# Transposing q and k of every stage on TensorE, with three prepared and two transposed buffers

## The chip, the cores and the metric

The kernel runs on one core of one Trainium2 chip. The metric is the device time of one execution in microseconds (us); the time given for a kernel is the median of several executions. A profiled execution has a time of its own, and inside it a span, from its first to its last recorded instruction.

## The reference

Two computations follow each other. The first is a linear attention with a decaying state, for 4 batches and 8 heads, 768 time steps, head dimension 48:

```python
for t in range(S):
    kt, vt, rt = k[:, :, t], v[:, :, t], r[:, :, t]
    cur = einsum('bhd,bhe->bhde', u[None] * kt, vt)
    y[:, :, t] = einsum('bhd,bhde->bhe', rt, state + cur)
    state = w[None, :, :, None] * state + einsum('bhd,bhe->bhde', kt, vt)
```

Its result, laid out as 3072 tokens of 384 numbers, goes through two dense layers with a leaky ReLU between them:

```python
h = x @ w_in                    # 3072 x 384 by 384 x 2048
g = maximum(0.01 * h, h)
out = g @ w_out                 # 2048 x 384
```

Inputs and output are float32; the kernel multiplies in bfloat16.

## The kernel before, in words

**Stages.** The time steps are cut into chunks of 128, six for each batch, so 24 stages `n` in all. A stage is one `front(n)` and one `back(n)`, and its loads are made by `load(n)`.

- `load(n)` (L409 to L416) issues three loads of 128 x 384 float32, for r, k and v, into one of `NRAW` = 4 raw buffers each. All are issued from SyncE (SP). A load waits until the stage that used the raw buffer four stages earlier has read it. From stage `NXQ` on it has one wait more (L415, `after=`): for the k product of stage n - `GATE`, two stages earlier.
- `front(n)` multiplies r and k by decay tables on VectorE into `qk_h` (q at L424, k at L426), and casts v to bfloat16 on ScalarE (L428). `qk_h` and `v_sb` have `NPREP` buffers. VectorE then makes the bonus term of u: two products and a sum (L430, L432, L434), from which GpSimd makes `vs` (L436).
- q and k are then transposed into `qkT`, which has `NT` buffers. There are two ways, and `n < NXQ` (L448) chooses. The first is eight 128 x 128 TensorE transposes into the PSUM bank `p_t` (L445), then one ScalarE copy of 128 x 1024 to `qkT` (L450). There is one `p_t` bank. The second is one transposing DMA from SBUF to SBUF, issued from SP (L453).
- From `qkT` come eight matmuls of the chunk's own attention (L460), masked on VectorE in two instructions (L465). k and v give the chunk's state update (L473 on TensorE, L481, L484 and L486 on VectorE).
- `back(n)` multiplies q by the state (L495) and the masked attention by v (L501), both on TensorE. VectorE adds `vs` (L507), TensorE transposes the result (L511), and ScalarE writes it to `xT` (L516).

**The dense layers.** `g1` (L572, evicted with the leaky ReLU by ScalarE at L577) and `g2` (L592, evicted by ScalarE at L596, stored from SP at L598) work on token tiles: eight of 128 tokens, then four of 512. They take turns in `NMOE` = 3 PSUM banks, which the small transpose of L511 shares. Twelve ScalarE casts (L533) bring `w_in` to bfloat16 in the first stages; `w_out` is loaded with a cast from GpSimd (L538).

**Order of the work.** The program isn't run in the order of its text. Every operation has a duration that the author wrote down and a priority; `Prog.schedule` (L116) plays the program through with these and writes down one fixed order for each engine. Stage work has a priority of about 100 n, dense work of over 100000, so that TensorE takes dense work when no stage work is ready. On the chip each engine then keeps its order, and waits on semaphores. A change of one buffer count or of one route therefore gives all engines a new order.

Of the kernel before, what the change touches and what calls it, by code (L numbers as in the profile page):

```python
# [26 lines left out]
TILES = [(L * i, L) for i in range(NSMALL)] + [(512 * i, 512) for i in range(NSMALL // 4, 6)]  # L27
NRAW = 4
FILL = (0.0, 0.0, 215.0)
NT = 3  # L30
GATE = 2
NXQ = 8
NXY = 24
WIN_AT = [0, 1, 2, 3]
WOUT_AT = [3, 4, 5, 6]
CAST = [20, 118, 160, 218]
RANK = {"q": 2, "k": 3, "v": 4, "bonus": 5, "vs": 7, "T": 8, "Tev": 9, "A": 10, "mask": 11, "kv": 10, "Z": 12, "S": 12,
        "qs": 14, "av": 14, "y": 15, "xt": 16, "xev": 17}
NPREP = 4
NGT = 3  # L40
NOUT = 3
NMOE = 3
# [21 lines left out]
class Prog:  # L64
# [10 lines left out]
    def op(self, eng, fn, dur, prio, w=(), r=(), banks=(), dma=None, svc=0, lock=False, grp=None, after=()):  # L75
        o = Op()
        o.eng, o.fn, o.dur, o.prio, o.dma, o.svc, o.lock, o.grp = eng, fn, dur, prio, dma, svc, lock, grp
        if grp is not None:
            if eng == "PE" and grp.first is None:
                grp.first = o  # L80
            grp.last = o
        o.idx = len(self.ops)
        o.name = str(list(w)[:1])
        o.deps = set()
        o.raw = set()
        for k in after:
            o.deps.add(self.writer[k])
        for k in r:
            if k in self.writer:
                o.deps.add(self.writer[k])  # L90
                o.raw.add(self.writer[k])
        for k in w:
            if k in self.writer:
                o.deps.add(self.writer[k])
                if self.writer[k].dma or eng != "PE":
                    o.raw.add(self.writer[k])
            for x in self.readers.get(k, ()):
                o.deps.add(x)
                if eng != "PE":
                    o.raw.add(x)  # L100
        for k in r:
            self.readers.setdefault(k, []).append(o)
        for k in w:
            self.writer[k] = o
            self.readers[k] = []
        for b in banks:
            last = self.bank.setdefault(b, {})
            for e, x in last.items():
                if e != eng:
                    o.deps.add(x)  # L110
            last[eng] = o
        o.deps.discard(o)
        self.ops.append(o)
        return o
# [179 lines left out]
def bass_rwkv5_eagle__then__act_leaky_relu_kernel(nc, r, k, v, w, u, moe_w_in, moe_w_out, out):  # L294
# [3 lines left out]
    def SB(name, shape, dt=BF16):  # L298
        return ctx.enter_context(nc.sbuf_tensor(name, shape, dt))
# [28 lines left out]
    raw_v = [SB(f"raw_v{i}", [128, H, D], FP32) for i in range(NRAW)]  # L328
    v_sb = [SB(f"v_sb{i}", [128, H, D]) for i in range(NPREP)]
    qk_h = [SB(f"qk_h{i}", [128, 2, H, E]) for i in range(NPREP)]  # L330
    q_h = [t[:, 0, :, :] for t in qk_h]
# [4 lines left out]
    vs = [SB(f"vs{i}", [128, H, D], FP32) for i in range(2)]  # L336
    qkT = [SB(f"qkT{i}", [128, 2, NP, L]) for i in range(NT)]
    ATm = [[SB(f"ATm{i}_{p}", [128, NP, L]) for p in range(2)] for i in range(2)]
# [58 lines left out]
    for p in range(2):  # L397
# [4 lines left out]
                                      w_tab[:, :, :], ALU.mult), 490, -80, w=["uw"], r=["w", gu], grp=gu)  # L402
    for i in range(NPREP):
        op("DVE", lambda i=i: V.memset(q_h[i][:, :, D:E], 0.0), 100, -60 + i, w=[f"qpad{i}"])
# [4 lines left out]
    def load(n):  # L409
        b, c = divmod(n, NC)  # L410
        ri = n % NRAW
        for j, (x, raw, nm) in enumerate(((r, raw_r, "rr"), (k, raw_k, "rk"), (v, raw_v, "rv"))):
            src = x[b].rearrange("h t d -> t h d")[c * L:c * L + L, :, :]
            op("SP", lambda src=src, raw=raw: [SP.dma_start(raw[ri][:, :, :], src)], 650, order[0],
               w=[f"{nm}{ri}"], after=[f"k{(n - GATE) % NPREP}"] if n >= NXQ else [], dma=(f"{nm}{ri}", 16), svc=1000)  # L415
            order[0] += 1  # L416

    def front(n):
        b, c = divmod(n, NC)
        ri, pi, di = n % NRAW, n % NPREP, n % 2  # L420
        base = n * 100
# [17 lines left out]

        T, ti = qkT[n % NT], n % NT  # L440
        gt = Group("t")
        def tr():
# [4 lines left out]
            return last  # L447
        if n < NXQ:  # L448
            op("PE", tr, 450, base + RANK["T"], w=[gt], r=[f"q{pi}", f"k{pi}", f"qpad{pi}", f"kpad{pi}", "ident"], grp=gt)
# [39 lines left out]
    def back(n):  # L489
        b, c = divmod(n, NC)  # L490
        pi, di, sc, base = n % NPREP, n % 2, n % 3, n * 100
        T, ti, vv = qkT[n % NT], n % NT, v_sb[pi]
        def qs():
            for i in range(NP):
                last = PE.matmul(p_y[:, 2 * D * i:2 * D * i + 2 * D], T[:, 0, i, :], s_bd[sc][:, i, :],  # L495
                                 start=(i == 0), stop=False, skip_group_check=True)
            return last
# [164 lines left out]
```

## Time and profile before

| | before |
|---|---|
| executions | 185.98, 187.28, 187.28 us |
| median | 187.28 us |
| profiled execution, its own time | 185.98 us |
| its span | 184.3 us |
| TensorE busy | 162.6 us (88%) |
| VectorE busy | 113.7 us (62%) |
| ScalarE busy | 111.7 us (61%) |
| GpSimd busy | 25.7 us (14%) |
| granted TensorE clock, mean | 0.991 |

In what follows PE is TensorE, PEld its weight loads, DVE VectorE, ACT ScalarE, POOL GpSimd. A group of instructions is given by line, engine, operation and tiles, followed by its count, its busy time in us and the mean of one in ns, then the idle time of the engine before it with what ended that. The busy time of a TensorE instruction holds its way through the array, so that instructions in a row overlap: what one costs in a row is read from the starts, or from the chain of waits, which counts nothing twice.

### The profile page before, as it was taken

The numbers are of one execution on the slowest core, as the hardware profiler recorded it, in microseconds if no ns is written. First come the engines' busy times: TensorE is split into PE (matmuls) and PEld (weight loads), VectorE is DVE, ScalarE is ACT, GpSimd is POOL, SyncE is SP. The second block draws the span as 40 slices with busy tenths as digits, with TensorE's granted clock in tenths as the row PEclk, the third lists the DMA queues.
The fourth block names the chain that finished last, engine by engine and source line by source line (L and its number), as shares of the span: only waits on it lengthen the run. The fifth ranks groups of instructions, "written<-read, shape, count | busy, mean of one in ns | idle before, by whom it ended". The sixth has DMA issues, their size and how long they took to land.

```text
span 184.3 us, 3981 instructions
## 1 busy us (share of the span) xinstructions
PE 162.6 (88%) x1632; PEld 105.7 (57%) x1642; DVE 113.7 (62%) x242; ACT 111.7 (61%) x196; POOL 25.7 (14%) x36
## 2 busy tenths in 40 slices
PE   0448488796999999999998999999999999999993
PEld 0227367686976668875554555665645654466561
DVE  2388758795999899999999999998600000000000
ACT  3877998995864147556677678632895149912221
POOL 2011111222112111111111211223000000000000
PEclk9999979999999999999999999999999999999999
DMA  3999999999659999999999989797000220012122
GB/s 84 252 218 233 263 276 180 205 201 218 129 108 229 207 230 222 203 189 231 231 176 223 220 163 227 143 161 184 7 0 0 85 78 13 0 43 85 52 80 85
DMA packets 97988, 28.25 MB, mean 153 GB/s; under 512 B 92721, under 2 KB 95922, under 8 KB 97970
## 3 DMA queue, kind: packets, MB, share of 16 engines
q1 hardware_dynamic: 96976, 26.42, 66.2%
q0 software_dynamic: 576, 1.57, 5.1%
q8 instruction: 13, 0.21, 0.5%
q10 hardware_dynamic: 418, 0.00, 0.1%
q14 instruction: 5, 0.04, 0.1%
HBM read 20.65 MB, written 4.72 MB: 138 GB/s over the span
## 4 chain that ended last, share of the span: by engine, by line
PE 76%; ACT 13%; DMA 6%; DVE 2%; issue 1%
PE p_moe L592 34%; PE p_moe L572 29%; DMA raw_v<-in_v_dram 4%; ACT w_in_sb L533 4%; PE p_a L460 3%; ACT gS L577 2%; PE p_y L501 2%; PE p_y L495 2%; ACT qkT L450 2%; DMA w_tab<-in_w_dram 2%; PE p_moe L511 2%; PE p_t L445 1%; PE p_z L473 1%; PE p_moe L383 1%; ACT xT L516 1%
## 5 line engine op out<-in xcount | busy, mean ns | idle before, releaser
L572 PE MATMUL p_moe<-xT,w_in_sb 128*128 128x128 bf16 (+1 forms) x566 | 74.5, 277 | 5.0 <-ACT w_in_sb L533 2.7
L572 PEld LDWEIGHTS p_moe<-xT,w_in_sb 128*128 128x128 bf16 x576 | 41.5, 101 | 23.9 <-ACT w_in_sb L533 4.2
L592 PE MATMUL p_moe<-w_out_sb,gT 128*128 128x384 bf16 x256 | 44.5, 326 | 0.5 <-ACT gT L577 0.5
L577 ACT ACTIVATE gT<-p_moe 128x512 bf16<-128x512 f32 x64 | 38.2, 597 | 10.6 <-PE p_moe L572 8.2
L596 ACT ACTIVATE o_sb<-p_moe 128x384 f32<-128x384 f32 x24 | 11.8, 491 | 41.2 <-PE p_moe L592 41.2
L436 POOL TENSOR_TENSOR vs<-v_sb,s_b 128x384 f32<-128x384 bf16 x24 | 22.0, 917 | 93.4 <-DVE s_b L434 54.8
L592 PEld LDWEIGHTS p_moe<-w_out_sb,gT 128*128 128x128 bf16 x256 | 24.6, 98 | 16.7 <-ACT gT L577 0.6
L592 PE MATMUL p_moe<-w_out_sb,gS 128*128 128x384 bf16 x128 | 24.2, 326 | 0.0
L577 ACT ACTIVATE gS<-p_moe 128x512 bf16<-128x512 f32 x32 | 18.4, 603 | 2.7 <-PE p_moe L572 2.5
L507 DVE TENSOR_TENSOR y_sb<-p_y,vs 128x384 bf16<-128x384 f32 x24 | 13.3, 553 | 8.2 <-PE p_y L501 8.1
L465 DVE TENSOR_TENSOR ATm_0<-p_a,mask_f 128x512 bf16<-128x512 f32 x24 | 16.4, 685 | 2.1 <-PE p_a L460 1.8
L424 DVE TENSOR_TENSOR qk_h<-raw_r,qdec 128x384 bf16<-128x384 f32 x24 | 14.5, 604 | 4.2 <-DMA raw_r<-in_r_dram 4.2
L465 DVE TENSOR_TENSOR ATm_1<-p_a,mask_f 128x512 bf16<-128x512 f32 x24 | 16.3, 679 | 0.0
L426 DVE TENSOR_TENSOR qk_h<-raw_k,kdec 128x384 bf16<-128x384 f32 x24 | 15.9, 661 | 0.3 <-ACT wlm L398 0.3
L428 ACT ACTIVATE v_sb<-raw_v 128x384 bf16<-128x384 f32 x24 | 12.5, 521 | 4.8 <-DMA raw_v<-in_v_dram 4.8
L592 PEld LDWEIGHTS p_moe<-w_out_sb,gS 128*128 128x128 bf16 x128 | 11.6, 98 | 6.3
L516 ACT ACTIVATE xT<-p_moe 128x384 bf16<-128x384 bf16 x24 | 11.8, 490 | 4.6 <-PE p_moe L511 4.4
L533 ACT ACTIVATE w_in_sb<-gT 128x512 bf16<-128x512 f32 x12 | 12.7, 1131 | 1.2 <-DMA gT<-in_moe_w_in_dram 1.2
L434 DVE TENSOR_REDUCE s_b<-qku 128x8 f32<-128x384 bf16 x24 | 13.1, 546 | 0.3
L445 PE MATMUL p_t<-ident,qk_h 128*128 128x128 bf16 x64 | 5.7, 242 | 7.9 <-DVE qk_h L426 7.9
L460 PE MATMUL p_a<-qkT 64*128 64x128 bf16 x192 | 10.0, 226 | 2.3 <-ACT qkT L450 2.2
L432 DVE TENSOR_TENSOR qku<-qk,uw 128x384 bf16<-128x384 bf16 x24 | 11.0, 458 | 0.4
(43 smaller groups left out, 125.3 us busy)
## 6 DMA issues: line engine op xcount, KB each, us to landing
raw_r<-in_r_dram SPq DMA_DIRECT2D x24, 192.0 KB, 3.5
raw_k<-in_k_dram SPq DMA_DIRECT2D x24, 192.0 KB, 4.0
raw_v<-in_v_dram SPq DMA_DIRECT2D x24, 192.0 KB, 4.1
out_dram<-o_sb SPq DMA_DIRECT2D x24, 192.0 KB, 2.0
gT<-in_moe_w_in_dram SPq DMA_DIRECT2D x4, 768.0 KB, 6.0
w_out_sb<-in_moe_w_out_dram POOLq DMA_DIRECT2D x4, 384.0 KB, 5.4
qkT<-qk_h SPq DMA_TRANSPOSE x16, 3.7
w_tab<-in_w_dram SPq DMA_DIRECT2D x1, 192.0 KB, 3.5
```

Source lines behind the costliest of these rows:

```text
L424: op("DVE", lambda: V.tensor_tensor(qh[:, :, 0:D], rr[:, :, :], qdec[:, :, :], ALU.mult), 490, base + RANK["q"], w=[f"q{pi}"], r=[f"rr{ri} ...
L426: op("DVE", lambda: V.tensor_tensor(kh[:, :, 0:D], rk_[:, :, :], kdec[:, :, :], ALU.mult), 490, base + RANK["k"], w=[f"k{pi}"], r=[f"rk{ri ...
L434: op("DVE", lambda: V.tensor_reduce(s_b[di][:, :], qku[di][:, :, :], AX.X, ALU.add), 470, base + RANK["bonus"], w=[f"s{di}"], r=[f"qku{di}"])
L436: op("POOL", lambda: G.tensor_tensor(vs[di][:, :, :], vv[:, :, :], s_b[di][:, :].unsqueeze(2).to_broadcast([128, H, D]), ALU.mult), 790, b ...
L460: last = PE.matmul(p_a[p][:, 128 * i:128 * i + 128], T[64 * p:64 * p + 64, 1, i, :], T[64 * p:64 * p + 64, 0, i, :], start=True, stop=True)
L465: op("DVE", lambda p=p: V.tensor_tensor(ATm[di][p][:, :, :], p_a[p][:, :].rearrange("p (i t) -> p i t", t=L), mask_f[:, :].unsqueeze(1).to ...
L507: op("DVE", lambda: V.tensor_tensor(y_sb[di][:, :], p_y[:, 0:DM], vs[di][:, :, :].rearrange("p h d -> p (h d)"), ALU.add), 490, base + RAN ...
L516: op("ACT", lambda: ACT.activation(xT[:, :, L * n:L * n + L], moe16(gx)[:, 0:DM].rearrange("p (m t) -> p m t", t=L), AF.Copy), 370, base + ...
L533: op("ACT", lambda m=m: ACT.activation(w_in_sb[:, m, CH * i:CH * i + CH].rearrange("p (j q) -> p j q", j=4), w_st[i][:, m, :].rearrange("p ...
L572: op("PE", lambda m=m, fb=fb, gr=gr: PE.matmul(p_moe[gr.bank][:, nt * (fb % per):nt * (fb % per) + nt], w_in_sb[:, m, 128 * fb:128 * fb + ...
L577: op("ACT", lambda f0=f0, gr=gr: ACT.activation(gb[:, f0:f0 + per, :], p_moe[gr.bank][:, :].rearrange("p (f t) -> p f t", t=nt), AF.Lrelu) ...
L592: op("PE", lambda q=q, fb=fb, gr=gr: PE.matmul(p_moe[gr.bank][:, 0:DM], gb[:, fb, 128 * q:128 * q + 128], w_out_sb[:, fb, :], start=(fb == ...
```

## The change

Three constants change:

```diff
-NT = 3
+NT = 2
 GATE = 2
-NXQ = 8
+NXQ = 24
 NXY = 24
...
-NPREP = 4
+NPREP = 3
```

`NXQ` = 24 is the number of stages. All stages now take the TensorE way of L445 and L450, where 16 took the transposing DMA of L453. The same constant switches the additional wait of the loads (L415): no stage has it any more, and a load waits for its raw buffer alone. `NT` = 2 leaves two buffers for the transposed q and k, and `NPREP` = 3 leaves three for the prepared q, k and v (the loop of padding memsets at L403 runs three times instead of four). What is computed does not change. Since the order of every engine is planned anew, dense and stage work are interleaved in another way from stage 7 on.

## The prediction

> **What bounds the kernel now.** I read the page first (busy shares), then busy time by stretch, then the waits, then the chain of waits.
>
> ```profile
> 0.00:46.00 46.00, 28.48 (x409) 23.36 (x409) 31.03 (x76) 36.38 (x54) 8.72 (x18) 0.96 0.98 213
> 46.00:52.00 6.00, 5.87 (x113) 5.49 (x113) 5.67 (x12) 5.53 (x11) 1.66 (x2) 1.00 0.62 124
> 52.00:130.40 78.40, 77.42 (x814) 48.91 (x823) 74.65 (x152) 45.47 (x90) 15.37 (x16) 1.00 0.99 195
> 130.40:184.30 53.90, 50.80 (x302) 27.96 (x304) 2.31 (x4) 24.28 (x44) 0.00 (x0) 1.00 0.12 45
> ```
>
> Columns: stretch, length, busy us (count) of PE, PEld, DVE, ACT, POOL, clock, DMA share, GB/s. Four regimes: a head in which PE idles; a short passage; stages 8 to 23, with PE (99%) and DVE (95%) both nearly full; and dense work alone, where PE has no gap. ACT is at 58% in the third.
>
> ```profile
> POOL vs L436 <- DVE s_b L434: 54.8, 13, 10.3
> ACT o_sb L596 <- PE p_moe L592: 41.2, 20, 2.9
> ...
> PE p_t L445 <- DVE qk_h L426: 7.9, 2, 7.2
> ACT v_sb L428 <- DMA raw_v<-in_v_dram: 4.8, 4, 2.1
> ...
> PE p_a L460 <- ACT qkT L450: 2.2, 4, 0.9
> ```
>
> These are waits: total us, times, longest. PE's own waits nearly all lie in the head; asked for 46 us onward, PE has only 0.5 and 0.2 us. No wait names the transposing DMA (L453): nobody stands visibly behind it.
>
> ```profile
> 49.00 0.20 PE p_y L501 x8
> 49.20 0.62 PE p_moe L572 x11
> 49.81 0.45 PE p_t L445 x8
> 50.26 0.17 PE p_z L473 x4
> ...
> 139.80 10.40 PE p_moe L592 x64
> 150.20 0.05 issue
> 150.25 10.31 PE p_moe L572 x47
> 160.56 20.82 PE p_moe L592 x128
> 181.37 0.02 issue
> 181.40 0.49 ACT o_sb L596
> ```
>
> From the chain of waits: from 46 us to the end it is PE in a row. One stage's eight transposes take 0.45 us there (56 ns each), and 64 dense matmuls of 384 columns take 10.40 us (163 ns). PE ends at 181.40; one eviction and one store follow, 2.9 us to the end of the span.
>
> **What the Trainium skill says.** "TensorE: Matmul & The Clock Gate", Part 4: PE-mode transpose, gives about 275 ns for a 128 x 128 transpose in a kernel. The trace's records (median 219 ns) are of that size, but they are latencies; in a row one costs 56 ns, which I use. "SBUF — State Buffer", Who interferes with whom, states that DMA never contends with a compute engine, so I expect no faster PE or DVE from fewer DMAs; the trace fits, with full-rate L592 matmuls at a DMA share of 1.0. The same section: a DVE instruction with two SBUF inputs contends with a GpSimd instruction that reads SBUF. The trace agrees: L432, 0.35 us alone, takes 0.87 us beside L436. "DMA: Bandwidth & Descriptors", Latency and other measured facts, gives 261 GB/s for transposing DMAs, an estimate of 1.0 us for the 262 kB of a stage; here it takes 3.7 us from issue to landing, so the measurement holds.
>
> **The change part by part.**
>
> *Transposes on PE.* 16 stages x 0.45 = 7.2 us more PE work. I listed both planned PE orders and priced each entry from the chain (L572 56 and 217 ns, L592 163, L501 25, L460 41, L495 and L473 43, transposes 55): 153.2 before, 160.2 us after, +7.0. There is no cover: PE has dense work waiting until the end.
>
> *Evictions on ACT.* 16 x 1.02 us (L450) = 16.4 us. ACT is busy 45.5 of 78.4 us in the third stretch; 61.9 of 78 (79%) fits. By the new order the tightest pair of stages (7 and 8) has about 4.4 us of ACT work between two transposed tiles, with DVE at about 4.3 to 5.7. Cost zero in the main case; if this cover fails, PE waits for L450, as in the head: 2.2 us in 4 of 8 stages, mean 0.28. Upper bound 16 x 0.28 = 4.4 us.
>
> *The DMA transposes leave.* 16 issues on SP, 1.3 to 3.8 us each, and 3.7 us of latency go. SP's loads and stores follow sooner. Nobody waited there, so the gain is nil in itself. What is late next: each stage now needs k product, transposes, L450, L460 in turn, about 0.45 + 1.02 + 0.4 us and handovers, near 2.1 us against 3.7.
>
> *The loads' second wait goes.* Stage 8's first load, issued at 41.25 us, could go at about 40.2, after stage 7's last. Behind loads that wait for reads of stage n - 4 stand stores on SP; three output buffers, with 2.6 us of PE work each, cover that. Gain between 0 and 2.1 us (the longest wait for `raw_v`, which belongs to stage 7, issued earlier): I take 0. The first transposing DMA comes at 56 us, so the head, where PE is idle, loses no work of any kind; up to stage 7's L460 (51.6 us) both PE orders are the same entry by entry.
>
> *Three and two buffers.* DVE can't work ahead as far. Before, it does so once: 11.3 us of PE work lie between the L460 of stages 7 and 8, with q and k of three stages done meanwhile. After, it is 3.5 us. So attention goes evenly, and DVE's pace counts in each stage. A full DVE stage takes 4.97 us in the trace (79.80 to 84.77, no gap). Pricing both DVE orders with the pieces of that stage (0.47 each for L424, L426, L484, L507; 0.6 for each L465; 0.46, 0.33, 0.28, 0.27 for L434, L430, L432, L486; 0.5 for the GpSimd block): from the masks of stage 7 to those of stage 23, 76.0 us before and 75.0 after. In the new order several L434 are followed by PSUM work that GpSimd doesn't block, so 73.3 is possible.
>
> *The sum.* In that same passage PE has 76.6 us of work before and 69.9 after: the planner, with a DVE stage of some 4.5 us, puts less dense work between the stages and leaves it for later (after the last L460: 51.0 before, 64.7 after). Taking for each stage the longer of PE and DVE: 79.9 before, where the trace has 78.75 (51.59 to 130.34), and 76.5 after. Less the same 1.1 us: 75.4. PE then idles 75.4 - 69.9 = 5.5 us against 78.75 - 76.55 = 2.2 before: +3.3 us. Last L460: 51.6 + 75.4 = 127.0; PE ends at 127.0 + 64.7 = 191.7; with 2.9 the span is 194.6, +10.3. On the profiled execution's own time, 185.98 + 10.3 = 196.3. The median, 187.28, stands 1.3 above; from it 197.6. Forecast **196.8**.
>
> **The rivals.**
>
> *PE's sum alone.* If DVE keeps ahead after all, PE stays full and only the 7.0 remain: 193.0 to 194.3. For it: PE has nearly no wait after 46 us today. Against it: DVE at 95% with nothing to spare.
>
> *A wait for the eviction takes the place of the DMA.* ACT takes dense evictions and L450 in one fixed order, and p_t is one bank. If every stage pays 0.28 us, and from this DVE also stands: +14.7, 200.7 to 202.0. For it: the head shows this wait. Against: there ACT was held up by the casts of w_in (1.1 us each), which are over by 35 us.
>
> *Faster.* The mechanism: loads without their second wait fill the head. PE is busy 28.5 of 39 us between 7 and 46; were all 10.5 idle us regained, 185.98 + 7.0 - 10.5 = 182.5. It decides only from 7 us on. Against: these are loads of stage 8 onward, issued from 41 us, while the head waits for stages 0 to 7, casts and a DMA share of 0.98. Also against a hidden gain: nothing in the third stretch is waiting for L453.
>
> *The change doesn't do what it says*: loads don't run ahead, since SP keeps its order behind loads that wait for DVE or ACT. It costs nothing here: 196.8 stays.
>
> **How the numbers follow.** Main case 0.53 (194.5 to 199), PE's sum 0.22, eviction waits 0.18, faster or equal 0.05, something slower still 0.02. The range holds the first two and the near part of the third: 193.0 to 201.0. A measurement of this kernel can tell about 1% from no change: slower by over 1% 0.93, within 1% 0.04, faster 0.03.
>
> **What would show it.** L450 x24, L445 x192, no transposing DMA. PE busy of dense-only work after the last L460 near 64 us; last L460 near 127 us; PE's waits for L450 and for DVE between 52 and 127 us summing to some 3 to 6 us; DVE still above 95% there. PE's sum is right if PE has no waits there and the last L460 comes by 124 us. Eviction waits are right if L460 <- ACT L450 tops PE's waits with over 4 us. I am wrong if the head gets shorter (stage 7's L460 well before 51.6), if L572 or L592 change their spacing, or if DVE needs less than 73 us for the sixteen stages.

## The result, and the profile after

The changed kernel takes 193.43 us in the median (192.99 to 194.00), the kernel before 187.28 (185.98 to 187.71) beside it: a ratio of 1.0342, with a 95% interval of 1.0281 to 1.0403. It is slower by about 6 us. In a later job the ratio was 1.0311 (1.0253 to 1.0369). Ratios leave out executions that took over 1.5% longer than the fastest of their kernel, so a ratio can differ a little from the quotient of the medians. The prediction, 196.8 in a range of 193.0 to 201.0, had the sign right, and its range holds the time; but the time that came is that of the rival "PE's sum alone", 193.0 to 194.3, near the lower edge of the range.

The profiled execution took 193.81 us, its span is 192.1, 7.8 more than before. Busy time by stretch, with the cuts set at the L460 of stage 7 and of stage 23 (columns as in the prediction: length; busy us of PE, PEld, DVE, ACT, POOL; clock; DMA share; GB/s):

```profile
0.00:46.00 46.00, 29.47 (x408) 24.65 (x409) 30.91 (x73) 36.48 (x54) 8.69 (x18) 0.93 0.96 210
46.00:52.94 6.94, 6.05 (x108) 5.27 (x106) 6.37 (x14) 5.29 (x11) 1.48 (x2) 1.00 0.85 168
52.94:124.53 71.59, 71.06 (x872) 48.87 (x880) 68.43 (x150) 54.38 (x96) 14.92 (x17) 1.00 0.66 140
124.53:192.10 67.57, 64.56 (x380) 35.70 (x381) 1.85 (x3) 29.87 (x54) 0.48 (x1) 1.00 0.13 47
```

The same passage, stage 7's L460 to stage 23's, of the kernel before:

```profile
51.59:130.34 78.75, 77.78 (x823) 49.16 (x829) 75.06 (x152) 45.81 (x91) 15.72 (x17) 1.00 0.98 195
```

So the passage with the attention stages has become 7.16 us *shorter*, and what lies behind it 13.61 us longer (67.57 against 184.30 - 130.34 = 53.96). The remaining +1.35 is the head: stage 7's L460 starts at 52.94 instead of 51.59 (followed up under "The wait put back into the changed kernel"). Together +7.80. PE is full in the passage, ACT is at 76%, the DMA share has fallen from 0.98 to 0.66, and DVE is busy for 68.4 us where it was busy for 75.1.

The waits of the changed kernel (us in total, times, longest):

```profile
POOL vs L436 <- DVE s_b L434: 87.6, 23, 10.3
ACT o_sb L596 <- PE p_moe L592: 36.7, 19, 2.4
...
PE p_t L445 <- DVE qk_h L426: 7.8, 2, 7.1
...
PE p_a L460 <- ACT qkT L450: 2.0, 3, 0.9
...
PE p_moe L511 <- DVE qku L432: 0.7, 1, 0.7
...
PE p_moe L572 <- issue: 0.3, 2, 0.2
```

The last two are all that PE waits for after 46 us. L460 waits for the ScalarE copy no more than before (2.0 us against 2.2), and all three of these waits lie before 46 us. The wait that was feared in place of the DMA did not come in the passage. GpSimd now always starts on L434; before, nine of its starts waited for L507.

The chain of waits ends as it did, with dense work in a row, only more of it:

```profile
128.33 0.17 PE p_moe L511 x3
128.49 8.78 PE p_moe L592 x54
137.27 0.05 issue
137.32 10.31 PE p_moe L572 x47
147.63 10.40 PE p_moe L592 x64
158.03 0.05 issue
158.08 10.31 PE p_moe L572 x47
168.39 20.82 PE p_moe L592 x128
```

47 matmuls of L572 in 10.31 us and 64 of L592 in 10.40 us are the same figures as before the change: the dense work itself costs what it did.

### The profile page after: what moved, and what is told of

It is laid out like the page before. It is cut to its first block, busy times and chain, and to the rows that moved or that the text cites. A ratio compares the mean times of both kernels' runs of the same rounds, so it can differ in the third digit from the quotient of the medians.

```text
span 192.1 us, 4241 instructions
## 1 busy us (share of the span) xinstructions
PE 171.1 (89%) x1762; PEld 114.5 (60%) x1770; DVE 107.6 (56%) x240; ACT 126.0 (66%) x212; POOL 25.6 (13%) x36
## 4 chain that ended last, share of the span: by engine, by line
PE 78%; ACT 11%; DMA 6%; DVE 3%; issue 1%
PE p_moe L592 33%; PE p_moe L572 29%; PE p_t L445 5%; DMA raw_v<-in_v_dram 4%; ACT w_in_sb L533 4%; PE p_a L460 3%; PE p_y L501 2%; PE p_y L495 2%; ACT qkT L450 2%; DMA w_tab<-in_w_dram 2%; ACT gS L577 2%; PE p_moe L511 2%; PE p_z L473 1%; DVE qk_h L426 1%; PE p_moe L383 1%
## 5 line engine op out<-in xcount | busy, mean ns | idle before, releaser
L572 PE MATMUL p_moe<-xT,w_in_sb 128*128 128x128 bf16 (+1 forms) x568 | 74.4, 279 | 4.4 <-ACT w_in_sb L533 3.1
L572 PEld LDWEIGHTS p_moe<-xT,w_in_sb 128*128 128x128 bf16 x576 | 42.3, 102 | 23.7 <-ACT w_in_sb L533 4.1
L592 PE MATMUL p_moe<-w_out_sb,gT 128*128 128x384 bf16 x256 | 42.4, 326 | 0.0
L577 ACT ACTIVATE gT<-p_moe 128x512 bf16<-128x512 f32 x64 | 37.7, 600 | 4.3 <-PE p_moe L572 2.3
L592 PEld LDWEIGHTS p_moe<-w_out_sb,gT 128*128 128x128 bf16 x256 | 24.9, 98 | 16.6
L436 POOL TENSOR_TENSOR vs<-v_sb,s_b 128x384 f32<-128x384 bf16 x24 | 21.8, 910 | 87.6 <-DVE s_b L434 87.6
L450 ACT ACTIVATE qkT<-p_t 128x1024 bf16<-128x1024 bf16 x24 | 24.6, 1023 | 8.2 <-PE p_t L445 7.9
L592 PE MATMUL p_moe<-w_out_sb,gS 128*128 128x384 bf16 x128 | 24.7, 326 | 0.0
L445 PE MATMUL p_t<-ident,qk_h 128*128 128x128 bf16 x192 | 15.9, 231 | 7.8 <-DVE qk_h L426 7.8
L445 PEld LDWEIGHTS p_t<-ident,qk_h 128*128 128x128 bf16 x192 | 13.0, 103 | 9.4 <-DVE qk_h L426 8.0
L465 DVE TENSOR_TENSOR ATm_0<-p_a,mask_f 128x512 bf16<-128x512 f32 x24 | 16.4, 684 | 3.2 <-PE p_a L460 3.2
L507 DVE TENSOR_TENSOR y_sb<-p_y,vs 128x384 bf16<-128x384 f32 x24 | 13.3, 554 | 7.4 <-PE p_y L501 7.2
L428 ACT ACTIVATE v_sb<-raw_v 128x384 bf16<-128x384 f32 x24 | 12.5, 523 | 5.5 <-DMA raw_v<-in_v_dram 3.3
L592 PEld LDWEIGHTS p_moe<-w_out_sb,gS 128*128 128x128 bf16 x128 | 11.3, 98 | 5.6
L426 DVE TENSOR_TENSOR qk_h<-raw_k,kdec 128x384 bf16<-128x384 f32 x24 | 14.2, 592 | 0.3 <-ACT wlm L398 0.3
L434 DVE TENSOR_REDUCE s_b<-qku 128x8 f32<-128x384 bf16 x24 | 13.1, 545 | 0.1
```

What stands on the lines that cost most here:

```text
L426: op("DVE", lambda: V.tensor_tensor(kh[:, :, 0:D], rk_[:, :, :], kdec[:, :, :], ALU.mult), 490, base + RANK["k"], w=[f"k{pi}"], r=[f"rk{ri ...
L434: op("DVE", lambda: V.tensor_reduce(s_b[di][:, :], qku[di][:, :, :], AX.X, ALU.add), 470, base + RANK["bonus"], w=[f"s{di}"], r=[f"qku{di}"])
L436: op("POOL", lambda: G.tensor_tensor(vs[di][:, :, :], vv[:, :, :], s_b[di][:, :].unsqueeze(2).to_broadcast([128, H, D]), ALU.mult), 790, b ...
L445: last = PE.transpose(p_t[:, 512 * x + 128 * i:512 * x + 128 * i + 128], t[:, 2 * i:2 * i + 2, :].rearrange("p h e -> p (h e)"), ident[:, :])
L450: op("ACT", lambda: ACT.activation(T[:, :, :, :].rearrange("p a i t -> p (a i t)"), p_t[:, :], AF.Copy), 910, base + RANK["Tev"], w=[f"T{t ...
L465: op("DVE", lambda p=p: V.tensor_tensor(ATm[di][p][:, :, :], p_a[p][:, :].rearrange("p (i t) -> p i t", t=L), mask_f[:, :].unsqueeze(1).to ...
```

## The experiments

Theory A: from 46 us on PE is always full, so the time moves by the PE work that is added or taken, 0.44 us for each stage transposed on TensorE (eight at the 55 ns of the prediction's prices), wherever the plan puts it. Theory B: the time comes from the buffers and from DVE's pace, with PE idle in the passage. The kernel before was run beside the others in every job; its median was 187.2 to 190.0 us by the job, so the ratios within a job are what is compared.

The table puts the runs together. "PE work" is the planned order priced as in the prediction; "idle" is the passage from stage 7's to stage 23's L460 in the profiled execution, less the PE work planned in it.

| kernel | PE work, us | passage - work = idle, us | ratio to before (95%) |
|---|---|---|---|
| before | 153.2 | 78.75 - 76.6 = 2.2 | 1 |
| buffers alone | 153.2 | 79.92 - 77.6 = 2.3 | 0.9985 (0.9958 to 1.0012) |
| TensorE in 16 stages | 156.7 | 75.83 - 73.3 = 2.5 | 1.0161 (1.0102 to 1.0220) |
| TensorE in 24, buffers of before | 160.2 | 71.60 - 69.9 = 1.7 | 1.0345 (1.0274 to 1.0417) |
| the whole change | 160.2 | 71.59 - 69.9 = 1.7 | 1.0342 (1.0281 to 1.0403) |
| the same, u product thrice | 160.2 | 79.90 - 78.0 = 1.9 | 1.0265 (1.0224 to 1.0306) |
| the same, transposes twice | 167.3 | 69.78 - 67.6 = 2.2 | 1.0623 (1.0485 to 1.0761) |
| loads' second wait alone | 153.2 | 82.97 - 74.6 = 8.4 | 1.0272 (1.0208 to 1.0336) |

Three more variants of the kernel before, described below, all with transposing DMAs, idle more than it in the passage, each by one profiled execution (190.22, 190.87 and 189.39 us): 80.46 - 75.3 = 5.2 us with a third `vs` buffer, 88.18 - 80.5 = 7.7 with `NXY` = 12, 78.38 - 70.3 = 8.1 with `NXQ` = 6. PE is full in the kernel before, but not in every variant of it.

### The parts of the change

**The route, with the buffers of before.**

```diff
-NXQ = 8
+NXQ = 24
```

> The kernel before with the TensorE transposes in all 24 stages and without the loads' second wait, but with its four prepared and three transposed buffers kept. Theory A (TensorE is full from 46 us on, and only the sum of its work counts): 6 to 7.5 us over the kernel before, the same as the whole change (+6.2 in medians). Theory B (the time comes from the buffers: with fewer of them VectorE can't work ahead and TensorE waits for it): at most 3 us over before.

193.89 us against 187.19: as slow as the whole change. What the change costs is in this constant, which switches both the route and the loads' second wait.

**Half of the route.**

```diff
-NXQ = 8
+NXQ = 16
```

> The kernel before with TensorE transposes in stages 0 to 15 and the transposing DMA in the last eight, buffers of before; loads of stages 8 to 15 without their second wait. Theory A: half of the sum, 8 x 0.45 = 3.6 us, so 2.8 to 4.4 us over before. Theory B, or any price that comes once with the change of the order: near 0 or near the full 6 to 7 us.

190.08 against 187.19 us; by the ratio +3.0 us, 1.9 to 4.1. Eight stages cost about half of what sixteen do, as a sum would, and no step in the cost shows.

**The buffers alone.**

```diff
-NT = 3
+NT = 2
-NPREP = 4
+NPREP = 3
```

> The kernel before, with DMA transposes from stage 8 on, with three prepared and two transposed buffers (the buffer part of the change alone). Theory A: no change of TensorE's work, so within 1 us of before. Theory B: 3 us or more over before.

187.13 against 187.19 us: no change. Even the long stretch of 11.3 us of PE work between the L460 of stages 7 and 8 is still in the plan, so that stretch did not come from the fourth prepared buffer, as the prediction had it, but goes with the transposing DMA. Theory B has lost its first half.

**The loads' second wait alone.**

```diff
-               w=[...], after=[f"k{(n - GATE) % NPREP}"] if n >= NXQ else [], ...
+               w=[...], after=[f"k{(n - GATE) % NPREP}"] if n >= NSTAGE else [], ...
```

> The kernel before with only the loads' second wait taken away (raw buffers alone hold the loads back), DMA transposes and buffers kept. Theory A: within 1 us of before, since no load is waited for after stage 8. Rival: loads issued earlier share the DMA engines with the loads of stage 7 and delay its L460 (51.6 us before, 52.9 after the change): +1 to +1.5 us, and stage 7's L460 above 52.5 us.

192.14 against 187.19 us: about 5 us slower, which neither theory had said. The PE work is that of before, but PE idles 8.4 us in the passage. The first transposing DMA is issued at 60.30 us instead of 56.13. SP's queue around it, with the loads that now stand ahead of it:

```profile
53.44 0.63 SPq L414 DMA_DIRECT2D raw_k<-in_k_dram  x1
54.11 1.63 SPq L414 DMA_DIRECT2D raw_v<-in_v_dram  x2
55.78 0.87 SPq L414 DMA_DIRECT2D raw_r<-in_r_dram  x1
56.69 1.42 SPq L414 DMA_DIRECT2D raw_k<-in_k_dram  x1
58.16 1.19 SPq L414 DMA_DIRECT2D raw_r<-in_r_dram  x1
59.39 0.86 SPq L414 DMA_DIRECT2D raw_k<-in_k_dram  x1
60.30 2.14 SPq L453 DMA_TRANSPOSE qkT<-qk_h  x1
```

And in the chain of waits of that kernel a transposing DMA stands in PE's way, which it never did before:

```profile
110.91 0.40 PE p_moe L592 x3
111.31 5.57 DMA qkT<-qk_h
116.87 0.05 issue
116.92 0.40 PE p_a L460 x8
```

The delay is not that of the first alone. From the end of the k product (L426) to the issue of the transposing DMA, stages 8 to 20 take 7.0 to 14.7 us here, and 1.8 to 5.7 in the kernel before. So in the kernel before, the second wait of the loads is worth about 5 us, and what it does in the trace is to keep loads that nobody needs yet from standing ahead of the transposes in SP's one queue. How much of the 5 us is the queue and how much the other plan (16.4 us of PE work between the L460 of stages 7 and 8, against 11.3) was not separated. In the changed kernel no transposing DMA is left to stand behind a load, and no such cost of the same removal shows: the route with its removal gives 6.5 us, the sum of PE work 7.0. The costs of the parts therefore don't add up: route and wait belong together.

**The wait put back into the changed kernel.**

```diff
-               ... if n >= NXQ else [], ...
+               ... if n >= 8 else [], ...
```

> The changed kernel with the loads' second wait put back from stage 8 on. If the earlier loads cost anything in the passage before stage 8: 1 to 1.5 us under the changed kernel, and stage 7's L460 back at 51.6 us. If that 1.3 us was the granted clock (0.69 between 35 and 40 us): within 0.7 us of the changed kernel.

194.21 against 190.01 us, ratio 1.0239 (1.0075 to 1.0403). The interval holds the changed kernel's ratio and one a good 2% below it, so this is inconclusive. Its profiled execution took 197.90 us, 3.7 over the median, with stage 7's L460 at 56.81 us, and can't say where that L460 belongs.

The later head can be followed in the traces instead. Two profiled executions of the changed kernel have stage 7's L460 at 52.94 and at 52.19 us. The first had a granted clock of 0.69 between 35 and 40 us, where the profile of before has 1.00, but that doesn't explain it: stage 6's L460 comes at 46.37 us, only 0.19 later than before, and most of the delay lies between the two. The chain of the changed kernel has there

```profile
43.17 7.28 DMA raw_v<-in_v_dram
...
50.47 0.52 ACT v_sb L428
51.00 0.97 ACT gS L577 x2
51.97 0.92 ACT qkT L450
...
52.94 0.40 PE p_a L460 x8
```

and that of the kernel before (starts in the chain can lie a few hundredths after those of the instructions)

```profile
50.60 1.06 PE p_moe L572 x19
51.66 0.33 PE p_a L460 x8
```

In the changed kernel's order of ACT, stage 8's cast of v (L428) stands ahead of stage 7's copy L450; in the kernel before it stands behind it. The cast waits for its load, and the copy with it. From stage 6's L460 to stage 7's it takes 5.41 us before and 6.57 and 5.62 in the two executions; the cast had waited 1.58 and 0.63 us. The two kernels with only the route constant changed have the same order and take 5.81 us (`NXQ` = 24, the cast waited 0.82) and 5.57 (`NXQ` = 16, 0.58), and the buffers alone, with the order of before, 5.41. So the new order costs the head 0.2 to 1.2 us, by when the load lands; why it lands later in one execution than in another is not shown.

### PE's sum or DVE's pace

**The transposes made twice.** In stages 8 to 23 the eight transposes of q and k are run a second time.

```diff
-                for i in range(NP):
+                for i in list(range(NP)) * (2 if n >= 8 else 1):
                     last = PE.transpose(p_t[...], t[...], ident[:, :])
...
-            op("PE", tr, 450, base + RANK["T"], ...
+            op("PE", tr, 900 if n >= 8 else 450, base + RANK["T"], ...
```

> The changed kernel, with the eight transposes of q and k done twice in stages 8 to 23 (128 matmuls more, same result), and planned at twice the time. Theory A: 16 x 0.45 = 7.2 us over the changed kernel, about 200.5 us (13.4 over before). Theory B (VectorE sets the pace of the stages and leaves TensorE idle there): part of it hides in the idle time, 2 to 4 us over the changed kernel.

201.15 against 190.01 us: 11.1 over before in the medians, 9.2 to 14.5 by the ratio's interval. The changed kernel stands 5.2 to 6.2 over before in its own two jobs, which would leave 5 to 6 us for 7.1 us of PE work. In this job it did not run itself, but two variants with its PE work did, at 193.10 and 194.21 us (the first try below and the wait put back), 7 to 8 us less; and between the spans lie 7.4 to 8.2 us (199.5 against 192.1 and 191.3). The interval alone would not rule out 4 us; the trace speaks against theory B: PE idles 2.2 us in the passage, against 1.7, so no idle time of PE was there to hide the work.

**More work for DVE, first try.** Two unused memsets in each stage.

```diff
+    dve_pad = SB("dve_pad", [128, 256], FP32)
...
+        if n >= 8:
+            for _ in range(2):
+                op("DVE", lambda: V.memset(dve_pad[:, :], 0.0), 270, base + RANK["bonus"], w=["dve_pad"])
```

> The changed kernel with two unused memsets of 128 x 256 float32 on VectorE in each of stages 8 to 23, planned at 270 ns each: estimated 16 x 0.5 = 8 us of VectorE work more, from the 0.27 us of the memset of that size in 32-bit words at the start of the trace. Theory A alone: within 1 us of the changed kernel. If VectorE has only 4 us of reserve between the L460 of stages 7 and 23 (70.4 busy of 75.0 us there), the stages take 4 us longer, and TensorE gets that much idle time unless the new plan puts dense work into it: 0 to 4 us, the last L460 at 128 us or later.

193.10 against 190.01 us, ratio 1.0231 (1.0102 to 1.0360): no cost shows, but it tells little. Nothing held the memsets to their stages, and the plan put 22 of the 32 ahead of stage 7, between 1.7 and 26 us.

**Second try, in the chain of the stage.** The u product is made three times, each waiting for the one before.

```diff
+        for _ in range(2 if n >= 8 else 0):
+            op("DVE", lambda: V.tensor_tensor(qku[di][:, :, :], qk[di][:, :, :], uw[:, :, :], ALU.mult), 270, base + RANK["bonus"],
+               w=[f"qku{di}"], r=[f"qk{di}", "uw"], lock=True)
```

> The changed kernel with the u product (L432) made three times instead of once in each of stages 8 to 23, each repeat in its stage's chain: 32 x 0.27 = 8.6 us of VectorE work more inside the passage between the L460 of stages 7 and 23 (VectorE 70.4 busy of 75.0 us there). Theory A in its bare form (TensorE alone counts, VectorE doesn't matter): within 1 us of the changed kernel. The prediction's mechanism (the longer of TensorE and VectorE counts in each stage) with the right size of VectorE's work: VectorE has some 4 us to spare there, the rest lengthens the passage: last L460 of stage 23 at 127.5 to 130 us. The new plan can put more dense work into the longer passage, as it plans the repeats too; then the time stays within 1.5 us of the changed kernel, and only otherwise does it rise by 3 to 5 us.

The passage of this kernel, stage 7's L460 to stage 23's:

```profile
52.80:132.70 79.90, 79.85 (x928) 53.75 (x927) 76.14 (x184) 58.05 (x102) 16.91 (x16) 1.00 0.62 132
```

It took 8.3 us longer than in the changed kernel and ended at 132.70 us, past the 127.5 to 130 expected, with DVE busy for 76.1 instead of 68.4 us. The time did not move all the same: 193.30 us, ratio 1.0265 (1.0224 to 1.0306), beside 194.06 and 1.0311 (1.0253 to 1.0369) for the changed kernel in the same job. The plan, which counts the repeats, had put 78.0 us of PE work into the longer passage instead of 69.9 and left as much less for the end, and PE idles only 1.9 us in it. So the planned length of DVE's work decided where dense work lies, and not how long the whole takes. Whether DVE would hold PE up where the plan has its durations too short was not tried.

**GpSimd at another place.** The kernel before with a third `vs` buffer.

```diff
-    vs = [SB(f"vs{i}", [128, H, D], FP32) for i in range(2)]
+    vs = [SB(f"vs{i}", [128, H, D], FP32) for i in range(3)]
...
```

L436 and L507 then use `vs[n % 3]` where they used `vs[di]`.

> The kernel before with three vs buffers in place of two, so that GpSimd (L436) no longer waits for L507 and runs at another place beside VectorE. If the 0.5 us of blocking per stage that the prediction put on VectorE comes from that place: VectorE busy falls by 3 to 7 us (113.7 before, 107.6 after the change), L432 falls from 458 to about 350 ns. Theory A: the time stays within 1 us all the same. If VectorE bounds the stages before: 2 us or more faster.

L432 in the kernel before, and with the third buffer (count, then the duration of one in ns, least, median and most):

```profile
L432 DVE TENSOR_TENSOR qku<-qk,uw x24: 343/349/867, 10.8 to 127.0; 128x384 bf16<-128x384 bf16 x24
```

```profile
L432 DVE TENSOR_TENSOR qku<-qk,uw x24: 345/357/359, 10.7 to 127.7; 128x384 bf16<-128x384 bf16 x24
```

In the kernel before five of the 24 take 0.87 us, each beside an L436. They are gone with the third buffer, as in the changed kernel (343/349/359), once GpSimd's L436 no longer starts on L507. Other lines of DVE are stretched in the same way: counted over the passage, eleven instructions before and three with the third buffer. DVE is busy 111.0 instead of 113.7 us, a smaller step than the change made (107.6). For the time this run decides nothing. The medians are 189.85 and 190.01 us, but one execution took 184.31, less than any of the kernel before in that job (lowest 187.46), and the other nineteen 187.74 to 191.87; no interval could be had for this pair. And in the profiled execution (190.22 us) two transposing DMAs stand in the chain of waits, which has none in the kernel before:

```profile
78.67 5.53 DMA qkT<-qk_h
...
93.20 5.84 DMA qkT<-qk_h
```

So what a relieved DVE is worth by itself stays open.

### Two tries at less PE work

**The last transposes by DMA.**

```diff
-NXY = 24
+NXY = 12
```

> The kernel before with the transposes of the attention's result (L511, three on TensorE, and its ScalarE copy L516) made by the transposing DMA from SP in stages 12 to 23. Theory A read the other way: 12 x 0.17 = 2.0 us less TensorE work, so 1.0 to 2.5 us faster than before. Rival (SP and the DMA engines have no room for twelve transposes more beside the sixteen of q and k): 1 us or more slower, with TensorE waiting between 75 and 135 us.

188.85 against 188.84 us, ratio 0.9984 (0.9949 to 1.0019): 2.0 us of PE work less, and no gain. Less PE work on paper helps only if PE stays full, and here the passage took 88.18 us for 80.5 us of work, 7.7 idle. That is from one profiled execution, of 190.87 us; most of what its waits name is L473 behind the cast of v (L428), 3.2 us in three waits. Whether the others wait like this is left open.

**The transposing DMA from stage 6.**

```diff
-NXQ = 8
+NXQ = 6
```

> The kernel before with the transposing DMA (and the loads' second wait) from stage 6 instead of 8. Theory A, if it held in the head too: 2 x 0.45 = 0.9 us faster, and ScalarE loses 2 us of L450 in the head, where it is nearly full. Rival: in the head TensorE has idle time, and the DMA engines are full (share 0.98), so the transposing DMAs queue behind the loads: no gain, or up to 4 us slower, with stage 7's L460 later than 52.5 us.

190.92 against 188.84 us, ratio 1.0036 (0.9996 to 1.0075): no gain. Stage 6's L460 starts at 54.18 us, against 46.18 in the kernel before: in the head, where the DMA engines are full (a share of 0.98 before), the first stage transposed by DMA comes later, and PE also idles 8.1 us in the passage. No version tried was shown to beat the kernel before.

## Why the prediction was right, and where it was off

The range held, but not through the main case (194.5 to 199, given 0.53): 193.43 lies in the part that was there for the rival, 0.4 us from the lower edge, so that the range held is owed to the rival and not to the main case's working. By the prediction's own signs, too, it is "PE's sum alone": the last L460 came at 124.53 us, half a microsecond after the "by 124 us" of the rival's sign and 2.5 before the 127 of the main case, PE was busy for 74.39 of the 75 us from 52 on, which leaves 0.6 us for waits where 3 to 6 were forecast, and DVE needed "less than 73 us for the sixteen stages", a sign named for being wrong.

- *Transposes on PE, +7.0, without cover.* Right within the noise: the ratios give 5.3 to 7.5 us for the whole change and 5.1 to 7.8 for the route with the buffers of before, and eight stages and the doubled transposes go with the sum. The spans of the two profiled executions are 7.8 and 7.0 over that of before, the first with the longer delay in the head.
- *The sum's idle time, +3.3.* This is the term that failed. The prediction had PE idle for "75.4 - 69.9 = 5.5" us in the passage; it was 71.59 - 69.9 = 1.7, less than the 2.2 before. Without this term the working gives 193.0 to 194.3, and 193.43 was measured.
- *Its cause: "0.5 for the GpSimd block".* I took the block from one stage of the trace (L432 at 0.87 us) and charged all sixteen, 8.0 us in all, although the listing of the new order said that several L434 would be followed by work that GpSimd doesn't block. In the passage of the kernel before eleven DVE instructions that run beside an L436 are longer than the median of their line by more than 30%, by 5.9 us together; in the changed kernel it is three, by 1.4 us. Without the block DVE's price is 67.0 us, less than PE's 69.9; DVE was busy for 68.4. Whether the longer of PE and DVE counts in each stage was not tested: in every variant of the changed kernel whose passage was priced PE was full in it, so nothing shows DVE holding it up.
- *Evictions on ACT, cost zero.* Right for the passage: 57.63 us busy in the 75 us from 52 on, and no PE matmul is listed as waiting for L450 after 46 us. In the head stage 7's L450 came late behind a cast.
- *The DMA transposes leave, gain nil.* Right: the DMA share in the passage fell by a third, and nothing got faster.
- *The loads' second wait, zero.* Nearly right for the change as it is made, for a reason that I had not seen: with the transposing DMA still there, its removal costs about 5 us. And I compared only PE's orders up to stage 7's L460; ACT's order differs there, at 0.2 to 1.2 us in the head.
- *Three and two buffers.* Their cost, nothing, is shown. My account of the 11.3 us stretch between stages 7 and 8 as work done ahead with the fourth buffer fell: three buffers keep it.
- *"PE's sum alone", given 0.22*, deserved more than the main case: PE had nearly no wait after 46 us, and the profile showed nothing stronger.

## What to carry to other kernels

Where one engine is full from some point to the end and other work can fill each gap, count first the work that the change puts on that engine; a second bound on top of it needs proof that the filler runs out there. This held here for work that was added; of the two tries to take work away neither gained, and in both traces the engine idled more. A duration stretched by contention belongs to the place where it was seen: check in the new order whether the two instructions still meet before charging it to each stage. Compare the new order of every engine, not only that of the full one. And a wait that looks like mere thrift, such as loads held back, may be what keeps a shared queue free for urgent work, so that its worth depends on what else that queue carries.

## What I had not expected of the hardware

Loads issued early on SP's queue delayed transposing DMAs that SP issued behind them, by four microseconds for the first (60.30 against 56.13 us); the kernel with these loads took about 5 us longer (ratio 1.0272), although the bytes moved were the same and the DMA share no higher (0.96 against 0.98). Eight TensorE transposes of 128 x 128 in a row took 0.45 us wherever they stood in the chain between dense matmuls at a granted clock of 1.00. The first two groups, at 7 and 14 us of the kernel before, after PE had been idle, took 1.04 us, and one at 34.95 us of the changed kernel, in the stretch with a clock of 0.69, took 0.85.
